# Maxima of the scores by quarters of k, and fourteen more pairs of them in the front

## The chip, the cores and the metric

One core of a Trainium2 chip runs the whole program in one launch. The metric is the device time of that core in microseconds. The engines are TensorE (PE in the profile; PEld is its weight load), VectorE (DVE), ScalarE (ACT), GpSimd (POOL) and SyncE (SP), which here only issues DMAs.

## The reference

Two mixers of the same shape run on two inputs, and a gate per row mixes them. `A` is the real part of a two-dimensional Fourier transform, written as products with DFT matrices; `B` is full attention with 32 heads of 16 dimensions. S is 2048, D is 512, all in float32.

```python
x = A_x                                                   # [1, 2048, 512]
g = sigmoid((x * gate_w).sum(-1, keepdims=True))
a = einsum("bsd,ed->bse", x, dft_hid_re)
b = einsum("bsd,ed->bse", x, dft_hid_im)
y = einsum("ts,bse->bte", dft_seq_re, a) - einsum("ts,bse->bte", dft_seq_im, b)

q, k, v = (B_x @ wqkv) split into 32 heads of 16
p = softmax(einsum("bhqd,bhkd->bhqk", q, k) * 16 ** -0.5)
o = einsum("bhqk,bhkd->bhqd", p, v) @ wo
return g * y + (1 - g) * o
```

`B_x` and `A_x` come from the same draw, so both mixers work on one x. The weights `wqkv` and `wo` are drawn 64 times larger than the rest. So the scores are large, and the softmax needs the true maximum of each row before the exponential.

## The kernel before

**Number format and halves of the array.** Most products are taken in a format that keeps part of the mantissa, with each operand split into a high and a low part (`hi_lo`), so one product becomes three matmuls. The attention products and the DFT products contract over 64 rows of the array. Two such matmuls run at the same time, one on the upper and one on the lower half of the array. I call one such pair of 64-row matmuls a slot.

**Pairs of heads.** The 32 heads are handled as NP = 16 pairs. The rows of q and k of pair p stand in `qs[p % 2]` and `ks[p % 2]`, one head in partitions 0 to 63, the other in 64 to 127. `load_rows(p, c, cols)` brings them from DRAM with three DMAs on SP's queue, `load_q` does that for q and clears (for p > 1) the rows that will take the negated maxima.

**Two passes over the scores.** The first pass, `a_tile`, computes a tile of 128 queries by 512 keys on TensorE and DVE reduces it to one maximum per query (L246 and L248). There are 64 such tiles for each pair and head: 16 query blocks times 4 quarters of k. They run with the query block outside and the quarter inside. When the tiles of eight query blocks of both heads are done, `m_parts` reduces the four maxima of each query and splits them, and `m_rows` transposes them (L267) and stores them by DMA as extra rows of `qs`, four DMAs on SP and four on POOL. The second pass, `scores` (L788), then multiplies k with those extended rows, so that the product already has the maximum subtracted, and ACT takes the exponential (L789). A unit u is one block of 128 keys of one pair for one half of the queries; there are 32 units per pair and 512 in all. `values` multiplies the exponentials of two units with v (`pv`, L824). One ACT copy takes the sum out, and POOL adds it up.

**The front.** Stage 1 (up to 93 us of the profile) computes q and k for all heads and stores them in DRAM. Then come four rows of v alone (L362) and the fours: `four` computes four blocks of 128 rows with 48 matmuls in each, in four phases of twelve slots (L344). In phases 0 and 1 each block gets one half of its contraction, in phases 2 and 3 the other, in the other half of the array. The first matmul of phases 2 and 3 waits for a maximum of the phase before (`guard`). There are three fours for v, four fours for b (the imaginary part along the hidden dimension), and one at `wre` for the first rows of a. In the first seven, `maxima` puts a pair of tiles, one for each head, behind the products 3 and 8 of each phase. That is 8 pairs in a four and `LEAD` = 56 in all. In the four at `wre`, `first_tiles` puts in scores and maxima. Banks of PSUM are taken in turn: four for the products of a four (`"s"`), and the other three and `psD` for the tiles (`"a"`).

**The segments.** From 209 us on, the work is written out as segments. A pattern is a string of slots: `s` is a score tile and `a` a tile of maxima, on one half of the array, while the other half works on a product of the DFT or of the output projection; a letter pair such as `aS` has tiles on both halves and no product. At `|` the plan is run, and the values of two units follow. Each pattern runs twice, with the halves exchanged, and the chains of products use `psD`. The order is 24 segments of `THIN` (the rest of a), 192 of `FULL` (the DFT along the sequence), and then the patterns of the projection: 14 segments of `FOURTEEN`, 2 of `TWELVE` and 16 of `TEN`, and the end.

```python
    FULL = "s a s s a a s s a a s a s a a s |"
    THIN = "aS s a s a s s a s a s a a sA |"
    FOURTEEN = ("aS s aS s a s ^ a s a s a sA |",) * 2
    TWELVE = ("sA a s a s ^ s a s a s s a s |",) * 2
    TEN = "aA s s a s ^ s s s a a sS |", "a s a sS a ^ s s s s s aA |"
```

In `FULL` a segment has eight scores and eight maxima; in `FOURTEEN` seven maxima, in `TWELVE` six and in `TEN` five. So the maxima keep their lead over the scores up to the projection, and it runs down there. The banks of score and maxima tiles come from a planner (`bank`, `read_by`), which guesses when each of seven banks will be free and takes the earliest; its first guesses are the list `free[:]` behind the four at `wre`.

**The plan.** `at(u, f, ...)` puts a step down for the end of the segment at which the values have come to unit u. The loads of pair p stand there relative to u = 32 * (p - 1): before the change q's first half 12 units ahead, the first half of k 6 ahead, the rest of k 4 and 2 ahead (the last quarter for each head by itself) and q's second half 2 ahead. DMAs issued by SP leave in program order, the loads of the DFT matrices (`c_load`, L392) among them.

Of the kernel before, what the change touches and what calls it, by code (L numbers as in the profile page):

```python
# [10 lines left out]
F32 = mybir.dt.float32  # L11
# [5 lines left out]
P = 128  # L17
S = 2048
D = 512
H = 32  # L20
DH = 16
NP = H // 2
KT = D // P
NT = S // P
UNITS = NP * 32
LEAD = 56
RAW = 6
PSUM = bass.MemoryType.PSUM
DRAM = bass.MemoryType.DRAM
# [3 lines left out]
def mix_kernel(ctx: ExitStack, tc: tile.TileContext, xa_t, xa, wqkv, w_hid, w_seq, wo, gate_w, out):  # L33
# [40 lines left out]

    xab = [const.tile([P, 4, 2, D], F32R, name=f"xab{tb}", tag=f"xab{tb}") for tb in range(4)]

    turns = dict.fromkeys("fsa", 0)

    def turn_of(kind):

        group = {"f": banks, "s": banks[:4], "a": [*banks[4:], psD]}[kind]
        turns[kind] += 1
        pool = group[(turns[kind] - 1) % len(group)]
        return pool.tile([P, 512], F32, name="d" if pool is psD else "t")
# [125 lines left out]

    PARTS = (0, 0, 1), (0, 1, 0)

    def load_rows(p, c, cols, heads=(0, 1)):


        t = (qs, ks)[c][p % 2]
        h0, n = heads[0], len(heads)
        rows = slice((2 * p + h0) * DH, (2 * p + h0 + n) * DH)
        for i, v in enumerate(PARTS[c]):
            nc.sync.dma_start(t[64 * h0 + i:64 * (h0 + n):4, cols].bitcast(F32), qk_d[c][v, rows, cols])  # L220

    def clear(t, rows, cols):
        dst = t[rows, cols].bitcast(F32).rearrange("r (n c) -> r n c", c=P)
# [6 lines left out]
            clear(qs[p % 2], slice(3, P, 32), cols)  # L230

    LOW, HIGH = slice(0, S // 2), slice(S // 2, S)
    THIRD, LAST = slice(S // 2, 3 * S // 4), slice(3 * S // 4, S)
    ALL = slice(0, S)


# [2 lines left out]

    def a_tile(i, h, ps=None):  # L240
        p, j = divmod(i, 64)
        qt, kb = divmod(j, 4)
        if ps is None:
            ps = turn_of("a")
        r = slice(64 * h, 64 * h + 64)
        nc.tensor.matmul(ps, qs[p % 2][r, qt * P:(qt + 1) * P], ks[p % 2][r, kb * 512:(kb + 1) * 512],  # L246
                         start=True, stop=True)
        user = nc.vector.tensor_reduce(mx[p % 2][:, h, qt, kb:kb + 1], ps, AX.X, ALU.max)  # L248
        n = 4 if p == NP - 1 and j >= 32 else 8
        k = qt // n  # L250
        a_left[p, n, k] = a_left.get((p, n, k), 8 * n) - 1
        if not a_left[p, n, k]:
            deferred.extend((partial(m_parts, p, n, k), partial(m_rows, p, n, k)))
        return user
# [24 lines left out]
    ones = st1.tile([4, 2 * D], F32, name="hl", bufs=2)  # L279
    nc.gpsimd.memset(ones, 1.0)  # L280
    for i in range(2):
        (nc.gpsimd if i else nc.vector).memset(ks[i].bitcast(F32), 0.0)
        nc.gpsimd.memset(qs[i].bitcast(F32), 0.0)
        if i == 0:
            load_rows(0, 1, ALL)
            load_q(0, ALL)
            nc.gpsimd.memset(vt[:, :, :, 16:17], 1.0)
        for tb in range(2):
            nc.gpsimd.dma_start(ks[i][3:P:32, tb * 2 * D:(tb + 1) * 2 * D].bitcast(F32), ones)
# [13 lines left out]
    def v_done(s, ps):  # L303

        pv = ps.rearrange("p (r h d) -> p r h d", h=2, d=DH)
        nc.scalar.copy(vt[:, s, :, 0:16], pv[:, :, 0])
        nc.vector.tensor_copy(vt[:, s, :, 17:33], pv[:, :, 1])
        if s in range(6, 14, 2):
            kt = (s - 6) // 2
            wt = st1.tile([P, 2, D], F32R, name="hl", bufs=2)  # L310
            hi_lo(wt[:, 0], wt[:, 1], wos.pop(0), nc.gpsimd)
            nc.sync.dma_start(wo_d[kt], wt.bitcast(F32))
            wrs.append(staged(w_hid[0, :, kt]))
# [19 lines left out]
    def four(ss, wh, wl, done, between=None):  # L333

        ps = [turn_of("s") for _ in ss]
        seen = None
        for phase, pair in enumerate(((0, 1), (2, 3), (1, 0), (3, 2))):
            guard, seen = seen, None
            both = [row_products(ss[c], wh, wl) for c in pair]
            for j in range(12):  # L340
                for half, c in enumerate(pair):
                    st, mv = next(both[half])
                    r = slice(64 * half, 64 * half + 64)
                    i = nc.tensor.matmul(ps[c], st[r], mv[r], start=phase < 2 and j == 0, stop=phase > 1 and j == 11)  # L344
                    if phase > 1 and j == 0:
                        tc.add_manual_dep(
                            i.ins, guard.ins.name,
                            mybir.DependencyInfo(mybir.DependencyClass.Sync, mybir.DependencyReason.DATA))
                if j in (3, 8):
                    user = between(phase, j) if between else maxima()  # L350
                    seen = seen or user
            if deferred:
                deferred.pop(0)()
            if phase > 1:
                for c in sorted(pair):
                    done(ss[c], ps[c])
# [417 lines left out]
    def scores(u, qb, h, ps=None):  # L774
        p, r = divmod(u, 32)
        hf, kt = divmod(r, 16)
        q0 = hf * 1024 + qb * 512
        if u >= UNITS - 16:

            blk, kt = divmod(kt, 8)  # L780
            q0, kt = 1024 + blk * 512, 2 * kt + qb
        if u not in pts:
            pts[u] = work.tile([P, 4, 512], F32, name="pt", bufs=4)
        if ps is None:
            i, ps = bank()
            read_by(i, "s")
        rr = slice(64 * h, 64 * h + 64)
        nc.tensor.matmul(ps, ks[p % 2][rr, kt * P:(kt + 1) * P], qs[p % 2][rr, q0:q0 + 512], start=True, stop=True)  # L788
        return nc.scalar.activation(pts[u][:, 2 * qb + h], ps, AF.Exp, bias=0.0, scale=DH ** -0.5)  # L789
# [94 lines left out]
    def at(u, f, *args):  # L884
        plan.setdefault(u, []).append(partial(f, *args))

    for p in range(2, NP):
        u = 32 * (p - 1)
        at(u - 12, load_q, p, LOW)
        at(u - 6, load_rows, p, 1, LOW)  # L890
        if p > 2:
            at(u - 4 if p < NP - 1 else u - 2, load_rows, p, 1, LAST, (1,))
        at(u - 4, load_rows, p, 1, THIRD)
        at(u - 2, load_rows, p, 1, LAST, (0,))
        at(u - 2, load_q, p, HIGH)

    for hf in range(2):
# [30 lines left out]

    FULL = "s a s s a a s s a a s a s a a s |"
    THIN = "aS s a s a s s a s a s a a sA |"  # L930
    FOURTEEN = ("aS s aS s a s ^ a s a s a sA |",) * 2
    TWELVE = ("sA a s a s ^ s a s a s s a s |",) * 2
    TEN = "aA s s a s ^ s s s a a sS |", "a s a sS a ^ s s s s s aA |"

# [31 lines left out]
    def segment(pattern, half, ds, stop, between=None, hold=True):  # L966


        nonlocal now
        nonlocal users  # L970
        before, users = users, []
        ds, late = iter(ds), []
        back = late if hold else None
        for n, slot in enumerate(pattern.split()):
            if slot == "|":
                for f in late:
                    f()
# [12 lines left out]
            if ahead:  # L990
                score(slot[0], 1 - half)
            if len(slot) == 1:
                x = next(ds, None)
                if x:

                    before = before if x[0].begun else None
                    i = issue(x, half, stop, back)
                    users = []
                    if before:
                        tc.add_manual_dep(  # L1000
                            i.ins, dict(before[::-1]).get("s", before[0][1]).ins.name,
                            mybir.DependencyInfo(mybir.DependencyClass.Sync, mybir.DependencyReason.DATA))
                        before = None
            if not ahead and slot != "d":
                score(slot[0], 1 - half)
            if len(slot) == 2:
                score(slot[1].lower(), half)
            if n == 1 and valued == 30:
                load_rows(2, 1, LAST, (1,))
        if deferred:  # L1010
            deferred.pop(0)()

    def pairs():

        for i in range(NT - 4):
            yield (THIN,) * 2, take(hid, 12)
        for i in range(2 * NT * 3):
            yield (FULL,) * 2, take(seq, 16)
        for patterns, n in ((FOURTEEN, 7), (TWELVE, 1), (TEN, 8)):
            for i in range(n):  # L1020
                yield patterns, take(both_first, 9)

# [14 lines left out]
    def first_tiles(phase, j):  # L1037

        if j == 3:
            user = scores(*next(streams[0][0]), turn_of("a"))  # L1040
            a_tile(*next(streams[1][1]))
            return user
        for h in range(2):
            a_tile(*next(streams[h][1]))

    four(range(4), *wre, first_rows, first_tiles)
    free[:] = 0.0, 0.0, 4.0, 4.0, 1.0, 2.0, 3.0
# [59 lines left out]
```

## Time and profile before

| | us |
|---|---|
| median of 3 runs | 1673.14 (1672.26 to 1673.52) |
| the profiled execution | 1673.48 |
| its span, first to last instruction | 1671.6 |
| TensorE busy | 1661.8 (99% of the span) |
| DVE busy | 1379.8 (83%) |
| ACT busy | 1245.5 (75%) |
| POOL busy | 754.4 (45%) |
| granted TensorE clock | 0.999 |

The span is the time from the first to the last instruction in the profile, and the rest of the time lies around it. A share is an average over stages: front (104 to 197 us for the seven fours), THIN up to about 343 us, FULL up to about 1456 us, and the patterns of the projection behind it. What a change is worth is read stage by stage. In the chain that ended last, each row gives its start, its length and the work it belongs to; the rows of L824 mark the ends of segments.

### The profile page before, as it was taken

Reading aid. Unit: us, or ns where it says so; the run is one execution under the profiler, and the core shown is the slowest. Engines: PE = TensorE matmul, PEld = TensorE weight load, DVE = VectorE, ACT = ScalarE, POOL = GpSimd, SP = SyncE. Lnnn points to the kernel's source line nnn. Section 1 sums busy time; section 2 is a strip of 40 time slices with the busy share of each in tenths; the row PEclk is TensorE's granted clock in tenths of the full one; section 3 lists DMA queues with packets and bytes.
Section 4 is the critical chain, followed back from the end, with each engine's and each line's share of the span. In section 5 each row is a group of like instructions: output and inputs, shape, how many; then the busy total and the mean of one; then the engine's idle time right before and its main releaser. Section 6 shows DMA issues by size and latency. Waiting matters only on the chain.

```text
span 1671.6 us, 34975 instructions
## 1 busy us (share of the span) xinstructions
PE 1661.8 (99%) x13170; PEld 1000.6 (60%) x13170; DVE 1379.8 (83%) x2299; ACT 1245.5 (75%) x2470; POOL 754.4 (45%) x813
## 2 busy tenths in 40 slices
PE   9999999999999999999999999999999999999998
PEld 7889966655555555555555555555555555555554
DVE  5468788888888888888888888888888888888786
ACT  5212288887777788777777788777787788888995
POOL 1123644544444465454444556545455465422331
PEclk9999999999999999999999999999999999999999
DMA  9953401113121323212226333222232334531113
GB/s 302 338 156 133 164 2 38 29 49 87 53 64 56 87 80 118 68 59 65 74 80 239 95 103 110 77 68 75 55 99 57 89 112 118 196 129 32 23 51 134
DMA packets 88833, 165.65 MB, mean 99 GB/s; under 512 B 21056, under 2 KB 22472, under 8 KB 87512
## 3 DMA queue, kind: packets, MB, share of 16 engines
q1 hardware_dynamic: 84024, 162.63, 30.9%
q8 instruction: 104, 1.70, 0.4%
q0 software_dynamic: 4352, 0.39, 0.2%
q14 instruction: 65, 0.53, 0.1%
q10 hardware_dynamic: 288, 0.39, 0.1%
HBM read 107.73 MB, written 54.52 MB: 97 GB/s over the span
## 4 chain that ended last, share of the span: by engine, by line
PE 98%; DMA 1%; DVE 0%; SPq 0%; ACT 0%; issue 0%; DVEq 0%
PE d L457 36%; PE t L824 28%; PE t L246 12%; PE t L788 10%; PE t L344 5%; PE t L93 2%; PE t L91 2%; PE t L92 2%; PE t L805 1%; PE t L457 1%; DMA qs<-qk 0%; DMA raw<-wqkv 0%; DVE mx L248 0%; PE t L183 0%; DVE yp L649 0%; SPq L220 0%
## 5 line engine op out<-in xcount | busy, mean ns | idle before, releaser
L248 DVE TENSOR_REDUCE mx<-t 128x1 f32<-128x512 f32 x2016 | 1253.6, 684 | 217.6 <-PE t L246 178.9
L789 ACT ACTIVATE pt<-t 128x512 f32<-128x512 f32 x2048 | 1033.9, 632 | 9.9 <-PE t L788 9.5
L788 PE MATMUL t<-qs,ks 64*128 64x512 f32 x2048 | 739.9, 410 | 0.1
L246 PE MATMUL t<-ks,qs 64*128 64x512 f32 x2016 | 687.5, 398 | 1.0 <-DMA qs<-qk 1.0
L457 PE MATMUL d<-xab,ch 64*128 64x512 f32 x2016 | 656.0, 400 | 0.0
L824 PE MATMUL t<-pt,vt 128*32 128x512 f32 x3968 | 477.1, 598 | 0.0
L457 PEld LDWEIGHTS d<-xab,ch 64*128 64x128 f32 x2016 | 357.9, 184 | 141.8 <-issue 97.2
L246 PEld LDWEIGHTS t<-ks,qs 64*128 64x128 f32 x2016 | 365.3, 184 | 86.3 <-ACT pt L789 47.4
L788 PEld LDWEIGHTS t<-qs,ks 64*128 64x128 f32 x2048 | 369.0, 184 | 76.4 <-DVE mx L248 43.7
L457 PE MATMUL d<-xab,cl 64*128 64x512 f32 x1008 | 403.6, 400 | 0.0
L839 POOL TENSOR_TENSOR osum<-osum,oe 128x512 f32<-128x512 f32 x217 | 279.5, 1288 | 134.3 <-ACT oe L833 131.0
L833 ACT COPY oe<-t 128x512 f32<-128x512 f32 x217 | 127.4, 587 | 223.9 <-PE t L824 222.3
L824 PEld LDWEIGHTS t<-pt,vt 128*32 128x32 f32 x3968 | 103.6, 109 | 231.6 <-issue 148.9
L402 POOL CAST ch<-craw 128x512 fp32r<-128x512 f32 x126 | 77.3, 613 | 340.8 <-PE t L788 266.0
L457 PEld LDWEIGHTS d<-xab,cl 64*128 64x128 f32 x1008 | 185.7, 184 | 72.3 <-issue 50.3
L403 POOL TENSOR_TENSOR cl<-craw,ch 128x512 fp32r<-128x512 f32 x126 | 162.3, 1288 | 10.2
L271 POOL DMA_DIRECT2D qs<-mt x132 | 73.6, 563 | 98.4 <-DVE mt L267 82.4
L457 PE MATMUL d<-wo_hl,o_hl 64*128 64x512 f32 x288 | 76.5, 394 | 0.0
L457 PE MATMUL d<-wre,xab 64*128 64x512 f32 x288 | 70.0, 389 | 0.4 <-DVE mx L248 0.4
L457 PEld LDWEIGHTS d<-wo_hl,o_hl 64*128 64x128 f32 x288 | 51.3, 184 | 10.2 <-ACT pt L789 6.7
L457 PEld LDWEIGHTS d<-wre,xab 64*128 64x128 f32 x288 | 53.0, 184 | 3.8 <-DVE mx L248 0.8
L91 PE MATMUL t<-xab,wh 128*128 128x512 f32 x124 | 48.2, 389 | 0.0
(118 smaller groups left out, 951.2 us busy)
## 6 DMA issues: line engine op xcount, KB each, us to landing
craw<-w_seq SPq DMA_DIRECT2D x128, 256.0 KB
qk<-hl SPq DMA_DIRECT2D x32, 512.0 KB
qs<-qk SPq DMA_DIRECT2D x84, 128.0 KB
b<-hl SPq DMA_DIRECT2D x16, 512.0 KB
xab<-b SPq DMA_DIRECT2D x16, 512.0 KB
o<-osum SPq DMA_DIRECT2D x62, 128.0 KB
oh<-nh SPq DMA_DIRECT2D x12, 512.0 KB
o_hl<-oh SPq DMA_DIRECT2D x6, 1024.0 KB
```

Source lines behind the costliest of these rows:

```text
L91: nc.tensor.matmul(ps, sh, mh, start=first, stop=False)
L246: nc.tensor.matmul(ps, qs[p % 2][r, qt * P:(qt + 1) * P], ks[p % 2][r, kb * 512:(kb + 1) * 512], start=True, stop=True)
L248: user = nc.vector.tensor_reduce(mx[p % 2][:, h, qt, kb:kb + 1], ps, AX.X, ALU.max)
L344: i = nc.tensor.matmul(ps[c], st[r], mv[r], start=phase < 2 and j == 0, stop=phase > 1 and j == 11)
L402: nc.gpsimd.tensor_copy(h1, raw)
L403: nc.gpsimd.tensor_tensor(l1, raw, h1.bitcast(F32), ALU.subtract)
L457: i = nc.tensor.matmul(self.ps, st[r], mv[r], start=not self.begun, stop=stop)
L788: nc.tensor.matmul(ps, ks[p % 2][rr, kt * P:(kt + 1) * P], qs[p % 2][rr, q0:q0 + 512], start=True, stop=True)
L789: return nc.scalar.activation(pts[u][:, 2 * qb + h], ps, AF.Exp, bias=0.0, scale=DH ** -0.5)
L824: nc.tensor.matmul(acc[32 * j:32 * j + 32], vt[:, kt, p, h:h + 32], pt[:, j], start=u == us[0], stop=u == us[-1])
L833: nc.scalar.copy(oe, acc)
L839: nc.gpsimd.tensor_tensor(o, o, oe, ALU.add)
```

## The change

Six things change together.

1. `a_tile` runs the tiles with the quarter of k outside and the query block inside, over groups of eight query blocks (four in the second half of the last pair).
2. The loads of k go by quarters of the keys, both heads together: the quarters 14, 10, 6 and 2 units ahead. q's first half is loaded 14 units ahead in place of 12.
3. In the seven fours, the pairs of maxima stand behind the products 2 and 7 of phase 0, 1, 5 and 10 of phases 1 and 3, and 3 and 8 of phase 2. That is 10 pairs in a four, and `LEAD` is 70. With those of the four at `wre`, the lead at the first segment is 74 tiles for one head and 78 for the other.
4. In the projection, the 14 segments of `FOURTEEN` go, and 14 more of `TEN` come: 2 of `TWELVE`, then 30 of `TEN`.
5. The tiles in the four at `wre` take three banks in turn, without `psD`.
6. The second copy of v leaves DVE for ACT, and of the first two memsets of `ks` and `qs`, `ks` goes to POOL and `qs` to DVE.

```diff
-LEAD = 56
+LEAD = 70
...
-        group = {"f": banks, "s": banks[:4], "a": [*banks[4:], psD]}[kind]
+        group = {"f": banks, "s": banks[:4], "a": [*banks[4:], psD], "r": banks[4:]}[kind]
...
-    def load_rows(p, c, cols, heads=(0, 1)):
+    def load_rows(p, c, cols):
         t = (qs, ks)[c][p % 2]
-        h0, n = heads[0], len(heads)
-        rows = slice((2 * p + h0) * DH, (2 * p + h0 + n) * DH)
+        rows = slice(2 * p * DH, 2 * (p + 1) * DH)
         for i, v in enumerate(PARTS[c]):
-            nc.sync.dma_start(t[64 * h0 + i:64 * (h0 + n):4, cols].bitcast(F32), qk_d[c][v, rows, cols])
+            nc.sync.dma_start(t[i:P:4, cols].bitcast(F32), qk_d[c][v, rows, cols])
...
     def a_tile(i, h, ps=None):
         p, j = divmod(i, 64)
-        qt, kb = divmod(j, 4)
+        n = 4 if p == NP - 1 and j >= 32 else 8
+        k, j = divmod(j, 4 * n)
+        kb, qt = divmod(j, n)
+        qt += n * k
...
     for i in range(2):
-        (nc.gpsimd if i else nc.vector).memset(ks[i].bitcast(F32), 0.0)
-        nc.gpsimd.memset(qs[i].bitcast(F32), 0.0)
+        nc.gpsimd.memset(ks[i].bitcast(F32), 0.0)
+        (nc.gpsimd if i else nc.vector).memset(qs[i].bitcast(F32), 0.0)
...
         nc.scalar.copy(vt[:, s, :, 0:16], pv[:, :, 0])
-        nc.vector.tensor_copy(vt[:, s, :, 17:33], pv[:, :, 1])
+        nc.scalar.copy(vt[:, s, :, 17:33], pv[:, :, 1])
...
-                if j in (3, 8):
+                if j in (((2, 7), (1, 5, 10), (3, 8), (1, 5, 10))[phase] if not between else (3, 8)):
                     user = between(phase, j) if between else maxima()
...
     for p in range(2, NP):
         u = 32 * (p - 1)
-        at(u - 12, load_q, p, LOW)
-        at(u - 6, load_rows, p, 1, LOW)
-        if p > 2:
-            at(u - 4 if p < NP - 1 else u - 2, load_rows, p, 1, LAST, (1,))
-        at(u - 4, load_rows, p, 1, THIRD)
-        at(u - 2, load_rows, p, 1, LAST, (0,))
+        at(u - 14, load_q, p, LOW)
+        for kb in range(4):
+            at(u - 14 + 4 * kb, load_rows, p, 1, slice(kb * 512, (kb + 1) * 512))
         at(u - 2, load_q, p, HIGH)
...
-            if n == 1 and valued == 30:
-                load_rows(2, 1, LAST, (1,))
...
-        for patterns, n in ((FOURTEEN, 7), (TWELVE, 1), (TEN, 8)):
+        for patterns, n in ((TWELVE, 1), (TEN, 15)):
...
         if j == 3:
-            user = scores(*next(streams[0][0]), turn_of("a"))
-            a_tile(*next(streams[1][1]))
+            user = scores(*next(streams[0][0]), turn_of("r"))
+            a_tile(*next(streams[1][1]), turn_of("r"))
             return user
         for h in range(2):
-            a_tile(*next(streams[h][1]))
+            a_tile(*next(streams[h][1]), turn_of("r"))
```

More of the change, by code (lines that the diff above doesn't have):

```diff
@@ L75, in mix_kernel @@
     xab = [const.tile([P, 4, 2, D], F32R, name=f"xab{tb}", tag=f"xab{tb}") for tb in range(4)]
-    turns = dict.fromkeys("fsa", 0)
+    turns = dict.fromkeys("fsar", 0)
     def turn_of(kind):
-        group = {"f": banks, "s": banks[:4], "a": [*banks[4:], psD]}[kind]
+        group = {"f": banks, "s": banks[:4], "a": [*banks[4:], psD], "r": banks[4:]}[kind]
         turns[kind] += 1
@@ L232, in mix_kernel @@
     LOW, HIGH = slice(0, S // 2), slice(S // 2, S)
-    THIRD, LAST = slice(S // 2, 3 * S // 4), slice(3 * S // 4, S)
     ALL = slice(0, S)
@@ L248, in a_tile @@
         user = nc.vector.tensor_reduce(mx[p % 2][:, h, qt, kb:kb + 1], ps, AX.X, ALU.max)
-        n = 4 if p == NP - 1 and j >= 32 else 8
-        k = qt // n
         a_left[p, n, k] = a_left.get((p, n, k), 8 * n) - 1
@@ L930, in mix_kernel @@
     THIN = "aS s a s a s s a s a s a a sA |"
-    FOURTEEN = ("aS s aS s a s ^ a s a s a sA |",) * 2
     TWELVE = ("sA a s a s ^ s a s a s s a s |",) * 2
```

## The prediction

> **What bounds the kernel now.** I read the page first (busy times and the chain that ended last), then that chain in order of time to get the period of each stage, then DVE's timeline where a stage is longer than its matmuls, and last the timelines of the entry of the front and of the load queue.
>
> ```profile
> span 1671.6 us, 34975 instructions
> ...
> PE 1661.8 (99%) x13170; PEld 1000.6 (60%) x13170; DVE 1379.8 (83%) x2299; ACT 1245.5 (75%) x2470; POOL 754.4 (45%) x813
> ...
> PE 98%; DMA 1%; DVE 0%; SPq 0%; ACT 0%; issue 0%; DVEq 0%
> ...
> L248 DVE TENSOR_REDUCE mx<-t 128x1 f32<-128x512 f32 x2016 | 1253.6, 684 | 217.6 <-PE t L246 178.9
> ...
> L246 PE MATMUL t<-ks,qs 64*128 64x512 f32 x2016 | 687.5, 398 | 1.0 <-DMA qs<-qk 1.0
> ```
>
> TensorE issues all the time, so a gain comes only where its stream is stretched: by empty half-slots, or by a matmul that waits for a bank. The chain gives the stretch stage by stage. A slot here is one pair of 64-row matmuls, one on each half of the array.
>
> ```profile
> 125.71 0.23 PE t L246 x2
> 125.94 1.13 PE t L344 x10
> ...
> 128.89 0.23 PE t L246 x2
> ...
> 190.49 0.23 PE t L246 x2
> ...
> 192.12 1.64 PE t L344 x14
> 193.76 0.23 PE t L246 x2
> ```
>
> In the front a phase is 12 product slots and 2 maxima slots. In the three v fours it lasts 128.89 - 125.71 = 3.18 us and a slot 1.13 / 5 = 0.226 us; in the four b fours 3.27 us and 1.64 / 7 = 0.234 us. There are no holes: the front runs at its matmuls.
>
> ```profile
> 1450.14 1.85 PE t L824 x16
> 1455.95 1.85 PE t L824 x16
> ...
> 1482.98 1.85 PE t L824 x16
> ...
> 1531.25 1.85 PE t L824 x16
> ...
> 1541.49 1.85 PE t L824 x16
> 1546.25 1.88 PE t L824 x16
> ...
> 1574.96 1.87 PE t L824 x16
> ```
>
> Each row is the block of value products that ends a segment, so differences are segment periods. FULL: 5.81 us for 16 slots. FOURTEEN, the 14 segments from 1455.95 to 1531.25: 75.30 us, 5.38 each, for 12 slots. TWELVE: (1541.49 - 1531.25) / 2 = 5.12. TEN: (1574.96 - 1546.25) / 6 = 4.785 for 11 slots. FOURTEEN has four slots fewer than FULL and gains only 0.43 us; by FULL it should take 5.81 - 4 x 0.226 = 4.91. Something else stretches it, and DVE's timeline shows what:
>
> ```profile
> 1479.94 4.28 DVE L248 TENSOR_REDUCE mx<-t 128x1 f32<-128x512 f32 x7 [0.42 <-PE t L788]
> 1485.29 4.28 DVE L248 TENSOR_REDUCE mx<-t 128x1 f32<-128x512 f32 x7 [1.07 <-PE t L788]
> 1489.48 0.74 DVE L649 SCALAR_TENSOR_TENSOR yp<-d,omg,yp 128x512 f32<-128x512 f32 x1
> ```
>
> Seven maxima run back to back for 4.28 us, while the slots of that segment need only 5.38 less the 1.85 of the value block, 3.5. DVE is the limit inside the slots and idles (1.07 us) during the value block; TensorE waits for banks in between. TEN has five maxima (about 3.1 us) and lacks this wait. The same rows give DVE's pace: (4.28 - 0.68) / 6 = 0.60 us from one maximum to the next.
>
> **Part 1: fourteen pairs of maxima go to the front, FOURTEEN becomes TEN.** Each of the seven fours gets 10 pairs in place of 8, so LEAD goes from 56 to 70, and seven pairs of FOURTEEN segments (7 maxima per half) become TEN (5 per half): 14 pairs either way. In the tail, 14 TEN segments take 14 x 4.785 = 66.99 in place of 75.30: **-8.31 us**. At the least it saves the bare slot, 14 x 0.226 = 3.2, if the wait seen in FOURTEEN stays. I take the full figure since TEN ran at 4.785 from its first segments on, right behind TWELVE, and will again.
>
> In the front, TensorE pays the slots: 6 pairs x 0.226 + 8 x 0.234 = **+3.23 us**. That holds only if DVE keeps up. A v four will have 58 slots, 13.1 us, a b four 13.6; DVE has 20 maxima x 0.60 = 12.0. The copies of the v fours would not fit beside that:
>
> ```profile
> L307 DVE COPY vt<-t x16: 415/420/425, 98.9 to 145.0; 128x256 f32<-128x256 f32 x16
> ...
> L306 ACT COPY vt<-t x16: 379/388/391, 98.5 to 144.2; 128x256 f32<-128x256 f32 x16
> ```
>
> Four of 0.42 us in a four make 13.7, over the 13.1; the change gives them to ACT, where eight copies of 0.39 are 3.1 us in 13.1, so they cost nothing (left on DVE, about 3 x 0.6 = 1.8 us). The third pair is spread well: pairs are 5 to 7 slots apart, at worst 1.13 us against 1.20 of DVE work, and 7 slots follow. Each bank is used again two pairs later, at least 11 slots or 2.49 us, while a pair's second maximum ends about 0.43 + 0.60 + 0.68 = 1.7 us after its matmul (0.43 is the lag from a matmul to its maximum that DVE's rows show above, 0.42). The first product of phases 2 and 3 waits for the first pair of the phase before, 10 slots earlier: 2.27 against 1.7. What eats into this slack is the group maximum and its transpose, now twice inside the front:
>
> ```profile
> L259 DVE TENSOR_REDUCE nm<-mx x33: 186/209/220, 157.5 to 1629.3; 128x16 f32<-128x64 f32 x31, 128x8 f32<-128x32 f32 x2
> ...
> L267 DVE STREAM_TRANSPOSE mt<-nhl x33: 201/202/213, 161.2 to 1630.1; 128x32 f32<-128x32 f32 x33
> ```
>
> 0.41 us of lag per group against a slack of 0.6 to 0.8. I book **+0.3 us** for the front, between 0 and 0.8 (both groups in full). Their row stores (four DMAs on SP, four on POOL for each group) come earlier, too; POOL has room for the second group, which falls into the last b four:
>
> ```profile
> L271 POOL DMA_DIRECT2D qs<-mt x132 | 73.6, 563 | 98.4 <-DVE mt L267 82.4
> ...
> 193.59 0.61 POOL L320 CAST hl<-raw 128x512 fp32r<-128x512 f32 x1 [4.43 <-ACT raw L318]
> ```
>
> Four issues of 0.56 make 2.3 us beside an idle spell of 4.43, and the eviction behind them (b_done on POOL) holds no bank.
>
> A page of the Trainium skill speaks against this: "VectorE: DVE Perf Modes", section "The DRAIN you can't avoid", says that a VectorE operation does not start before the one ahead of it has emptied the pipe. With 684 ns for each maximum that would make 13.7 us of DVE per four, above TensorE's 13.1 and 13.6. This trace differs: seven maxima of 684 ns in 4.28 us overlap by about 0.08 each. I go by the trace and keep the rule as a rival.
>
> **Part 2: the entry of the front.** The two memsets ahead of the loads of pair 0 change engines.
>
> ```profile
> 93.21 1.81 POOL L283 MEMSET qs<- 128x2048 f32 x1 [41.31 <-PE t L92]
> ...
> 95.71 1.76 DVE L282 MEMSET ks<- 128x2048 f32 x1 [0.38 <-DMA qk<-hl]
> 97.50 1.80 SPq L220 DMA_DIRECT2D ks<-qk  x3
> ...
> 99.40 1.81 SPq L220 DMA_DIRECT2D qs<-qk  x3
> ...
> 104.18 1.20 PE L344 MATMUL t<-wv,xab 64*128 64x512 f32 x8
> ...
> 106.36 0.50 PE L246 MATMUL t<-ks,qs 64*128 64x512 f32 x2 [0.98 <-DMA qs<-qk]
> ```
>
> SP issues the k loads at 97.50, when DVE's memset of k ends (97.47), and the q loads behind them. DVE reaches that memset only after its evictions and gate rows, while POOL has stood idle for 41 us and starts at 93.21. With k on POOL, k is clear at 95.0 and its loads go out from about 95.1 (SP's last store before them is then out); q, cleared by DVE, is ready at 97.5. The last q load then leaves 1.9 us earlier, and if it lands as long after its issue as now, the first pair's data is there at about 104.4. TensorE gets there at 104.18 + 3 slots = 104.9 and today waits from 105.09 to 106.36: **-1.27 us**, at worst 0 if k's memory is not free before 95.7. Behind the two memsets POOL has the ones of vt, which wait for a store anyway.
>
> **Part 3: the entry of the segments.**
>
> ```profile
> 207.72 0.39 PE L246 MATMUL d<-ks,qs 64*128 64x512 f32 x1
> ...
> 208.57 0.39 PE L788 MATMUL t<-qs,ks 64*128 64x512 f32 x1
> ...
> 209.43 0.49 PE L457 MATMUL d<-wre,xab 64*128 64x512 f32 x1 [0.42 <-DVE mx L248]
> ```
>
> The first chain of the segments (L457) needs psD, which the last maximum of the four at wre (the d of 207.72) holds until DVE has read it; unhindered it would start a slot behind 208.57, at 208.80, 0.63 earlier. With three banks in turn psD is free. But 16 tiles over three banks end on the first of them, and the planner gives just that bank to the next score. That score will wait for the same maximum, so the wait moves down by one matmul: **-0.3 us**, between 0 and -0.63.
>
> **Part 4: order of maxima and loads of k.** The same 64 maxima per pair and head run, and the groups of eight query blocks complete at the same counts; only the inner order changes. k of a pair came in 12 loads (six of them just ahead of its use); now it comes in 12, three for each quarter, at 14, 10, 6 and 2 units ahead, all on SP, and each set waits for the last score on the quarter that it overwrites. Behind that wait on SP's queue stand the chunk loads of the DFT.
>
> ```profile
> 833.15 17.39 SPq L220 DMA_DIRECT2D ks<-qk  x9
> 850.64 0.53 SPq L392 DMA_DIRECT2D craw<-w_seq  x1
> ...
> 855.09 0.39 PE L246 MATMUL t<-ks,qs 64*128 64x512 f32 x1
> ```
>
> Today such a wait also lasts (nine loads spread over 17.39 us, a chunk load behind them), and no chunk is late. The third quarter, issued by 850.54, is read at 855.09 without a wait: it lands within 4.6 us. After the change the first maximum of a pair runs third in the third segment behind the load, 1.85 + 2 x 5.81 + about 1.4 = 14.9 us later; q's four loads (rows and clear) and the three of k take 7 x 0.62 = 4.3 to issue, so 8.9 to land: 6 us to spare. **0 us**, and if the cover fails the rival below tells the price. FULL keeps its patterns, and its 16 slots at 0.226 plus the value block and 0.3 between them make its 5.81, so I leave it there.
>
> **Sum.** -8.31 + 3.23 + 0.3 - 1.27 - 0.3 = -6.35 us against the profiled execution, 1673.48 us (span 1671.6 and 1.9 around it): 1667.1. The median of the runs shown is 0.34 below that execution: **1666.8 us**. With the best ends (0 for the front's lag, -1.27, -0.63) it is 1666.2; with both entries bringing nothing and 0.8 of lag it is 1668.9.
>
> **The rivals.**
>
> *DVE bounds the front* (the DRAIN rule at work as a mechanism: each maximum holds DVE for its 684 ns). Seven fours at 20 x 0.684 = 13.7 make 95.8 us, where the slots make 3 x 13.1 + 4 x 13.6 = 93.7: +2.1, so 1668.9. For it: six maxima in an odd phase are more than its slack allows one by one. Against it: the 4.28 us row. Chance 0.13.
>
> *The tail does not follow*: TEN brought forward runs into what stretches FOURTEEN, such as late projection operands, and only the bare slots are saved (3.2, not 8.3): 1666.8 + 5.1 = 1671.9, within 0.2% of no change. For it: the loads of the last DFT tile end just there. Against it: FOURTEEN's waits are for DVE, none for a load. Chance 0.12.
>
> *Slower: k's quarters come late.* Today's reader of a new pair is eight units later. If the landing takes over 14.9 us, q's loads being ahead of k's on SP, TensorE waits once in each of the 14 pairs from 2 to 15; the gain is gone at 6.35 / 14 = 0.45 us per pair, and it is slower by over 0.2% from 0.7 us on; a wait of 1.5 us gives 1666.8 + 21 = 1687.8. For it: the queue holds waits up to 17 us. Against it: 4.6 us to land, and only 1.0 us of waiting for loads in all of L246. Chance 0.11.
>
> **Numbers.** What is left, 0.64, is for the sum as it stands. Measurement of this kernel tells about 0.2%, 3.3 us, from no change. Faster by more takes the main case and most of the DVE rival (1668.9 is 4.2 under the median): 0.64 + 0.12 = 0.76; same takes the second rival and the rest: 0.13; slower 0.11. The range goes from 1664.8 (the best ends, less 1.4 for FULL periods that shift by 0.007 us over 192 segments) to 1670.0 (the DVE rival with 0.8 of lag, rounded up).
>
> **What would show it.** Right: b phases with two and three pairs alternate at 3.28 and 3.51 us without a DVE release in the chain; value blocks of the tail 4.785 apart from the third segment on; k loads issued near 95; no DMA in the chain at 105. Wrong: DVE mx L248 in the chain of the front, waits of L246 for qs<-qk once a pair, a FULL period other than 5.81, or tail segments over 5.

## The result: 1669.1 us in place of 1672.8, three fifths of the forecast gain

| | before | after |
|---|---|---|
| median of 13 runs each, us | 1672.78 (1671.93 to 1674.05) | 1669.10 (1668.11 to 1671.40) |
| span of the profiled execution, us | 1671.6 | 1667.9 |

The ratio is 0.9978, with a 95% interval of 0.9969 to 0.9986. So the changed kernel is faster, by 3.7 us. The forecast was 1666.8 us with a range of 1664.8 to 1670.0, and a gain of 6.35 us.

The first view of the changed kernel is its page: span, busy times, shares of the chain that ended last, and the group of the matmuls of the maxima (busy time and mean ns of one, then the idle time ahead of them with what ended most of it).

```profile
span 1667.9 us, 34971 instructions
...
PE 1658.0 (99%) x13170; PEld 984.6 (59%) x13170; DVE 1374.9 (82%) x2283; ACT 1251.0 (75%) x2486; POOL 753.4 (45%) x813
...
PE 98%; DVE 0%; POOL 0%; DMA 0%; issue 0%; SPq 0%; DVEq 0%; ACT 0%
...
L247 PE MATMUL t<-ks,qs 64*128 64x512 f32 x2013 | 675.6, 399 | 1.6 <-POOL qs L282 1.6
```

The shares say nothing about the difference: TensorE is still 99% busy. But one word is new. In the kernel before, the matmuls of the last row waited 1.0 us for a load of q. Now they wait 1.6 us for something on POOL. That leads to the step that failed.

The stage table is worked out from the chains of the two profiled executions, from one landmark to the next.

| stage, us | before | after | difference | forecast |
|---|---|---|---|---|
| up to the rows of v | 93.21 | 93.42 | +0.21 | 0 |
| rows of v | 10.97 | 10.97 | 0 | 0 |
| first product of the fours to the first pair of maxima | 2.17 | 2.53 | +0.36 | -1.27 |
| first pair to the first score of the segments | 102.21 | 105.51 | +3.30 | +3.53 |
| first score to the first block of values | 4.41 | 4.49 | +0.08 | -0.3 |
| `THIN` | 128.00 | 127.97 | -0.03 | 0 |
| `FULL` | 1114.90 | 1115.50 | +0.60 | 0 |
| the 32 segments of the projection | 162.67 | 154.50 | -8.17 | -8.31 |
| end | 53.04 | 53.05 | +0.01 | 0 |
| sum | 1671.59 | 1667.95 | -3.64 | -6.35 |

One slot has moved between two of these rows. The first pair of maxima stands behind four slots of products in the kernel before and behind three in the changed one. With that slot (0.23 us) taken into account, the way to the first pair grew by 0.59 and the stage behind it by 3.07.

The two large terms came out nearly as forecast. The tail is in the chain of the changed kernel, whose rows L823 end the segments:

```profile
1460.47 1.85 PE t L823 x16
...
1465.67 1.85 PE t L823 x16
...
1470.79 1.85 PE t L823 x16
...
1475.54 1.88 PE t L823 x16
```

Two segments of `TWELVE` take 5.20 and 5.12 us, and the first `TEN` behind them 4.75. From there on they are 4.785 apart, and 4.84 to 4.87 where a group maximum falls in. The last but one takes 5.21. That is what `TEN` took before (there the last but one took 5.20), now 30 times.

The front in the same chain, for ten pairs of maxima of a v four and then ten of a b four:

```profile
123.31 0.23 PE t L247 x2
...
136.46 0.23 PE t L247 x2
...
176.65 0.23 PE t L247 x2
...
190.11 0.23 PE t L247 x2
```

A v four takes 136.46 - 123.31 = 13.15 us and a b four 190.11 - 176.65 = 13.46, for 58 slots each. That is 0.227 and 0.232 a slot, and no row of DVE stands between them in the chain. DVE's timeline shows how close it is:

```profile
131.35 1.98 DVE L249 TENSOR_REDUCE mx<-t 128x1 f32<-128x512 f32 x3
133.24 0.68 DVE L249 TENSOR_REDUCE mx<-d 128x1 f32<-128x512 f32 x1
133.84 1.98 DVE L249 TENSOR_REDUCE mx<-t 128x1 f32<-128x512 f32 x3
135.74 0.68 DVE L249 TENSOR_REDUCE mx<-d 128x1 f32<-128x512 f32 x1
136.72 1.89 DVE L249 TENSOR_REDUCE mx<-t 128x1 f32<-128x512 f32 x3 [0.30 <-PE t L247]
```

Eight maxima take from 131.35 to 136.42, which is 0.63 each, and one starts before the one ahead of it ends (133.24 against 133.33). DVE hardly rests: in the three v fours together it waits 1.0 us for TensorE. And TensorE's waits show none for DVE in these fours.

The entry of the front went the other way. This is the timeline of the changed kernel (start, length, engine and line, and in brackets the idle time before with what ended it):

```profile
93.42 1.81 POOL L281 MEMSET ks<- 128x2048 f32 x1 [40.67 <-PE t L92]
...
94.96 0.36 SPq L144 DMA_DIRECT2D qk<-hl  x1
95.43 1.81 SPq L219 DMA_DIRECT2D ks<-qk  x3
...
95.92 1.76 DVE L282 MEMSET qs<- 128x2048 f32 x1 [0.38 <-issue]
97.71 1.72 SPq L219 DMA_DIRECT2D qs<-qk  x3
...
100.75 0.59 POOL L286 MEMSET vt<- 128x256 f32 x1 [5.52 <-DMA ks<-qk]
...
101.27 1.28 POOL L288 DMA_DIRECT2D ks<-hl  x2
...
106.93 0.50 PE L247 MATMUL t<-ks,qs 64*128 64x512 f32 x2 [1.57 <-POOL qs L282]
```

The loads of k leave at 95.43 and those of q at 97.71, as forecast (2.1 and 1.7 us earlier than before). But POOL then stands still for 5.52 us, until it clears `vt`, and behind that memset it issues the stores of ones into `ks` (L288), which the first pair of maxima needs as well. The same rows of the kernel before:

```profile
98.42 0.59 POOL L287 MEMSET vt<- 128x256 f32 x1 [3.40 <-DMA qk<-hl]
...
99.00 1.29 POOL L289 DMA_DIRECT2D ks<-hl  x2
```

There the ones left at 99.00, now at 101.27. The last row of the fence above names POOL's memset of `qs` as what released the first pair. That memset clears the other pair's `qs` and ended at 106.13, 0.8 us before the pair started, so another release is meant. The landing of the ones is the candidate, since the pair starts 5.7 us behind their first issue and the trace gives their two DMAs a median of 5.3 us from issue to landing; the first experiment tries it. What POOL waits for ahead of the memset of `vt` is named as a load of k here, and as the store `qk<-hl` in the kernel before and in the next two profiles quoted below. I take it to be the store, which the memset waits for in the kernel before too.

### The profile page after: what moved, and what is told of

The parts are those of the page before. It is cut to its first block, busy times and chain, and to the rows that moved or that the text cites. A ratio compares the mean times of both kernels' runs of the same rounds, so it can differ in the third digit from the quotient of the medians.

```text
span 1667.9 us, 34971 instructions
## 1 busy us (share of the span) xinstructions
PE 1658.0 (99%) x13170; PEld 984.6 (59%) x13170; DVE 1374.9 (82%) x2283; ACT 1251.0 (75%) x2486; POOL 753.4 (45%) x813
## 4 chain that ended last, share of the span: by engine, by line
PE 98%; DVE 0%; POOL 0%; DMA 0%; issue 0%; SPq 0%; DVEq 0%; ACT 0%
PE d L456 37%; PE t L823 28%; PE t L247 12%; PE t L787 9%; PE t L343 5%; PE t L93 2%; PE t L92 2%; PE t L91 2%; PE t L804 1%; PE t L456 1%; DMA ks<-qk 0%; PE t L161 0%; PE t L183 0%; DVE mx L249 0%; DVE yp L648 0%; PE t L733 0%
## 5 line engine op out<-in xcount | busy, mean ns | idle before, releaser
L787 PE MATMUL t<-qs,ks 64*128 64x512 f32 x2048 | 728.7, 408 | 0.4 <-DVE mx L249 0.2
L247 PE MATMUL t<-ks,qs 64*128 64x512 f32 x2013 | 675.6, 399 | 1.6 <-POOL qs L282 1.6
L823 PE MATMUL t<-pt,vt 128*32 128x512 f32 x3968 | 477.1, 598 | 0.0
L247 PEld LDWEIGHTS t<-ks,qs 64*128 64x128 f32 x2013 | 359.8, 184 | 84.2 <-ACT pt L788 55.9
L823 PEld LDWEIGHTS t<-pt,vt 128*32 128x32 f32 x3968 | 103.6, 109 | 232.1 <-issue 148.7
```

What stands on the lines that cost most here:

```text
L823: nc.tensor.matmul(acc[32 * j:32 * j + 32], vt[:, kt, p, h:h + 32], pt[:, j], start=u == us[0], stop=u == us[-1])
```

## Experiments

**The ones.** My theory after the result: the first pair waits for the stores of ones, and those stand on POOL behind the memset of `vt`, which waits for the last store of the stage before (`qk<-hl`). Put behind the ones, that memset costs nothing. The rival: the loads themselves land later, and the wait stays.

```diff
         if i == 0:
             load_rows(0, 1, ALL)
             load_q(0, ALL)
-            nc.gpsimd.memset(vt[:, :, :, 16:17], 1.0)
         for tb in range(2):
             nc.gpsimd.dma_start(ks[i][3:P:32, tb * 2 * D:(tb + 1) * 2 * D].bitcast(F32), ones)
+        if i == 0:
+            nc.gpsimd.memset(vt[:, :, :, 16:17], 1.0)
```

> The changed kernel, with the memset of the ones in vt put behind the two stores of ones into ks of pair 0 on POOL's queue. Theory: the first pair of maxima waits for these stores, which stand on POOL behind the vt memset, and that memset waits until the last store of stage 1 has landed (100.7). Then the stores leave near 95.3, the first pair runs at about 105.2 without a wait in place of 106.93, and all behind it is 1.7 us earlier. Rival: the loads of k and q themselves land late, because they now share the DMA engines with the last store; then the first pair stays at 106.9 and nothing is gained.

```profile
95.30 1.81 SPq L219 DMA_DIRECT2D ks<-qk  x3
...
95.41 1.29 POOL L287 DMA_DIRECT2D ks<-hl  x2 [0.30 <-POOL ks L281]
...
100.47 0.58 POOL L289 MEMSET vt<- 128x256 f32 x1 [3.78 <-DMA qk<-hl]
...
105.06 0.40 PE L247 MATMUL t<-ks,qs 64*128 64x512 f32 x2
```

This is its timeline. The ones leave at 95.41, the memset of `vt` still waits until 100.47, and the first pair runs at 105.06 without a wait. From the first product of the fours to the first pair it is 0.80 us, in place of 2.53, and 2.17 in the kernel before. The time was 1667.62 us. So the theory holds. Against the kernel before that is -1.37 as the rows stand and -1.14 with the moved slot, so Part 2 of the prediction (-1.27) would have been nearly right if this memset had not been in the way.

Timed over several runs, the same edit:

> The kernel of the run with the vt memset behind the stores of ones, timed against the kernel before. Theory: 1.7 us from the entry on top of the changed kernel, so about 5.4 us under the kernel before (ratio 0.9968); the profile shows the first pair at 105.2 at the latest. Rival: the single run was lucky in the landing of its loads, and the median stays within 0.7 us of the changed kernel (ratio 0.9974 to 0.9978).

1667.50 us, median of 7 runs (1666.86 to 1667.85), against 1672.57 for the kernel before on that chip; the ratio is 0.997 with an interval of 0.9958 to 0.9981. The wait of the first pair is again 0.80. This is the best version that I ran: 5.1 us under before. The interval overlaps that of the changed kernel (0.9969 to 0.9986), so that it is faster than that one rests on the entry in the profiles more than on these times.

**The swap of the memsets, undone.** With the old engines for `ks` and `qs`, first with the memset of `vt` where the change has it, then with it behind the ones.

```diff
-        nc.gpsimd.memset(ks[i].bitcast(F32), 0.0)
-        (nc.gpsimd if i else nc.vector).memset(qs[i].bitcast(F32), 0.0)
+        (nc.gpsimd if i else nc.vector).memset(ks[i].bitcast(F32), 0.0)
+        nc.gpsimd.memset(qs[i].bitcast(F32), 0.0)
```

> The changed kernel, with the first two memsets on the engines of before (ks on DVE, qs on POOL). Theory (stores of ones behind the vt memset): k's loads leave at 97.5 again, out of the way of the last store, which then lands near 98.4; the stores of ones follow at once, and the first pair runs at 106.3 to 106.6, 0.3 to 0.6 us earlier than in the changed kernel. Rival (the loads are the limit): k's loads leave 2.1 us later, so the first pair comes no earlier than 106.9 and rather later.

```profile
97.65 1.80 SPq L219 DMA_DIRECT2D ks<-qk  x3
98.58 0.59 POOL L286 MEMSET vt<- 128x256 f32 x1 [3.41 <-DMA qk<-hl]
...
99.16 1.28 POOL L288 DMA_DIRECT2D ks<-hl  x2
...
99.55 1.81 SPq L219 DMA_DIRECT2D qs<-qk  x3
...
105.61 0.50 PE L247 MATMUL t<-ks,qs 64*128 64x512 f32 x2 [0.31 <-DMA qs<-qk]
```

The first pair ran at 105.61, earlier than any theory had it. Loads that leave 2 us later landed early enough: in the chain, the last load of q takes 4.71 us to land here and 5.60 in the kernel before. In all 1668.23 us, from one run.

> The changed kernel with the vt memset behind the stores of ones and with the first two memsets on the engines of before. Theory: with the stores of ones out of the way the first pair waits for the loads, and these leave 2 us later when DVE clears k; so the first pair runs 0.4 to 1.3 us after TensorE could take it (between 105.5 and 106.4), where the kernel with the vt memset alone had no wait. Rival: the swap of the memsets does nothing once the stores of ones are early; the first pair then runs without a wait here too, about 0.8 us after the first product of the fours.

```profile
98.31 1.29 POOL L287 DMA_DIRECT2D ks<-hl  x2 [3.06 <-DVE ks L281]
...
99.63 1.81 SPq L219 DMA_DIRECT2D qs<-qk  x3
...
106.06 0.51 PE L247 MATMUL t<-ks,qs 64*128 64x512 f32 x2 [0.68 <-DMA qs<-qk]
```

Here the wait is for the loads of q, and the entry takes 1.65 us; in all 1668.59. The four combinations, with the time from the first product of the fours to the first pair in every profile that had that entry (some from the experiments below). The numbers marked with a star have four slots of products ahead of the pair, the others three:

| | memsets as before | memsets swapped |
|---|---|---|
| `vt` ahead of the ones | 2.17\*, 1.23\*, 1.74\*, 1.41\*, 1.28 | 2.53, 1.74, 2.00, 1.59 |
| `vt` behind the ones | 1.65 | 0.80, 0.80, 0.80 |

With 0.23 taken off the starred numbers for the slot that the others have behind the pair, the means of the upper row are 1.38 and 1.96. So by themselves the swapped memsets bring nothing and seem to cost 0.6, though the spreads overlap. Together with the earlier ones they bring about 0.85 (1.65, from one profile, to 0.80). And the spread of the starred numbers, 0.94 us with one and the same entry, says that my -1.27 was taken from a single landing at its slow end. Where the landing of q's last load stands in the chain with that entry, it takes 5.60, 5.17 and 4.84 us, and 5.60 is the profile that I had.

**Order of maxima and loads alone.** The kernel before, with the new order of tiles and loads by quarters only.

```diff
-        qt, kb = divmod(j, 4)
+        n = 4 if p == NP - 1 and j >= 32 else 8
+        k, j = divmod(j, 4 * n)
+        kb, qt = divmod(j, n)
+        qt += n * k
...
-        at(u - 12, load_q, p, LOW)
-        at(u - 6, load_rows, p, 1, LOW)
...
+        at(u - 14, load_q, p, LOW)
+        for kb in range(4):
+            at(u - 14 + 4 * kb, load_rows, p, 1, slice(kb * 512, (kb + 1) * 512))
```

> The kernel before, with only the order of the maxima (quarter by quarter over eight query blocks) and the loads of k by quarters at 14, 10, 6 and 2 units ahead; lead 56, FOURTEEN, memsets and copies as before. Theory: order and loads cost nothing by themselves; the stage FULL lasts 1114.9 us as before (within 0.1), no maximum waits for a load after the entry, and the whole is within 0.5 us of the kernel before. Rival: the order or the loads bring the two segments of 6.09 us that FULL shows in the changed kernel; then FULL is longer by about 0.56 here too.

1672.91 us, against 1672.57 for the kernel before beside it; `FULL` takes 1114.97 (before 1114.90), the 32 segments 162.58 (162.67). Part 4's 0 us holds for the reordering. One segment of `FULL` takes 6.09 us here, as two do in the changed kernel, and yet `FULL` as a whole grew by 0.07 only.

**The cover of the loads.** Is it 0 because the loads are hidden, or because such a load never matters? The changed kernel with k's loads four units later:

```diff
-            at(u - 14 + 4 * kb, load_rows, p, 1, slice(kb * 512, (kb + 1) * 512))
+            at(u - 10 + 4 * kb, load_rows, p, 1, slice(kb * 512, (kb + 1) * 512))
```

> The changed kernel, with the four loads of each pair's k four units later (10, 6, 2 units ahead and 2 behind), that is two segments or 11.6 us later. Theory: the cover of 14.9 us falls to 3.3 us, while three issues and the landing take about 1.9 + 4.6 = 6.5; the first maximum of a pair waits about 3 us, in most of the 14 pairs and again at later quarters, so the whole is 30 to 100 us slower. Rival: the loads land much faster than the bound of 4.6 us, and the loss stays under 10 us.

1711.72 us, inside the range that I had given; `FULL` grew by 43. The view of waits (engine, what it waited for, total us, times, longest) and two rows of the chain (start, length, what):

```profile
PE t L247 <- DMA ks<-qk: 25.9, 12, 2.8
```

```profile
492.24 2.52 DMA ks<-qk
...
680.22 2.24 DMA ks<-qk
```

So the slower rival's mechanism is real, and four units of lead stand between it and this kernel.

**The copies of v.** The changed kernel with the second copy of v left on DVE.

```diff
-        nc.scalar.copy(vt[:, s, :, 17:33], pv[:, :, 1])
+        nc.vector.tensor_copy(vt[:, s, :, 17:33], pv[:, :, 1])
```

> The changed kernel, with the second copy of v on DVE again, as before. Theory: DVE then has 20 x 0.60 + 4 x 0.42 = 13.7 us in a v four against 13.15 of slots; the three v fours take about 13.7 us each, 1.6 to 1.8 us more in all, with waits for mx in the chain. Rival: the copies run in gaps and four banks absorb the rest; the v fours stay at 13.15 us and nothing is lost.

1669.31 us. The front took 106.49 in place of 105.51, so the copies cost 0.98 us there, where I had said about 1.8. Its chain shows the place:

```profile
131.51 0.31 PE d L247
...
135.76 0.31 PE t L247 x2
```

A second tile that normally adds 0.01 us now adds 0.31. In the three v fours the weight loads of the maxima wait for DVE's maxima five times, 1.2 us in all, and never in the changed kernel. Sign and mechanism were right; DVE had more slack than I gave it.

**Which bank the first score takes.** In Part 3 I had the wait of the first chain move to the next score, which needs the same bank. Here the planner's first guesses give it another.

```diff
-    free[:] = 0.0, 0.0, 4.0, 4.0, 1.0, 2.0, 3.0
+    free[:] = 0.0, 0.0, 4.0, 4.0, 3.0, 1.0, 2.0
```

> The changed kernel, with the planner's first guesses changed so that the first bank of three, which the last maximum of the four at wre holds, is handed out last of the three (3, 1, 2 in place of 1, 2, 3). Theory: the wait moved from the chain's bank to the score's bank; then the score at 213.29 runs about 0.4 us earlier, and the way from the first score of the segments to the first value block falls from 4.49 us to about 4.0. Rival: DVE is behind by then in any case, and the wait moves on to the next tile: 4.4 to 4.5 us as in both kernels.

1668.74 us. From the first score to the first values it takes 4.46 in place of 4.49, so nothing was won: another wait, for DVE and then for ACT, takes its place. The chain of the changed kernel itself shows the wait that I had described:

```profile
211.82 0.10 PE t L247
...
211.95 1.30 DVE mx L249 x2
...
213.29 0.50 PE t L787
```

**What stretches `FOURTEEN`.** The prediction says DVE. The kernel before, with the maxima of these 14 segments taken over 256 of the 512 keys only:

```diff
-        user = nc.vector.tensor_reduce(mx[p % 2][:, h, qt, kb:kb + 1], ps, AX.X, ALU.max)
+        src = ps[:, :256] if short[0] else ps
+        user = nc.vector.tensor_reduce(mx[p % 2][:, h, qt, kb:kb + 1], src, AX.X, ALU.max)
...
+        short[0] = patterns is FOURTEEN
```

> The kernel before, with the maxima of the FOURTEEN segments taken over 256 of the 512 keys of a tile only (that part of the maxima is left out), so that each holds DVE for about 0.33 us in place of 0.60. Theory: FOURTEEN is stretched by tiles waiting for a bank that DVE still reads; with short maxima its period falls from 5.35 to 4.8 to 4.95 us, by 5.5 to 7.5 us over 14 segments. Rival: it is stretched by its pattern of slots on TensorE or by ACT; then it stays over 5.2 us.

1669.55 us. The 14 segments went from 75.30 to 72.22, a gain of 3.08 and well under what I expected; each still takes 5.16 in the chain. In these segments the weight loads of the maxima waited 11.4 us for DVE's maxima before, and 0.8 now. The timeline shows DVE resting and weight loads of the scores held by ACT:

```profile
1478.01 2.30 DVE L250 TENSOR_REDUCE mx<-t 128x1 f32<-128x256 f32 x5 [1.18 <-PE t L790]
...
1478.16 4.03 ACT L791 ACTIVATE pt<-t 128x512 f32<-128x512 f32 x8
...
1480.28 0.18 PEld L790 LDWEIGHTS t<-qs,ks 64*128 64x128 f32 x1 [0.19 <-ACT pt L791]
```

So the long maxima account for 3.08 of the 8.31 us by which the prediction has `FOURTEEN` above `TEN`. Another 3.2 is the bare slot that `FOURTEEN` has more (14 x 0.226), and about 2.0 are left. ACT was the next suspect: eight exponentials in 4.03 us and one copy of 0.59 make 4.62 in each segment. I moved that copy to DVE, on top of the short maxima, in `FOURTEEN` and `TEN`:

```diff
-        nc.scalar.copy(oe, acc)
+        (nc.vector.tensor_copy if on_dve[0] else nc.scalar.copy)(oe, acc)
...
+        on_dve[0] = patterns is FOURTEEN or patterns is TEN
```

> The kernel of the short maxima (before, with the maxima of FOURTEEN over 256 of 512 keys, the rest left out), and in FOURTEEN and TEN the copy of the value sums goes from ACT to DVE. Theory: what still stretches FOURTEEN there (5.15 us) and sets TEN (4.785) is ACT, with eight exponentials and one copy; without the copy ACT can start its exponentials earlier, and FOURTEEN falls to 4.85 to 4.95, TEN to 4.5 to 4.65. Rival: TensorE's own slots and the value block are the limit; both periods stay within 0.05.

1673.04 us. `FOURTEEN` fell to 71.22 only, 1.0 us less over 14 segments, and `TEN` rose from 4.785 to 5.03. The theory that ACT's share is what is left asked for 3 to 4 us in `FOURTEEN` and a shorter `TEN`, so it fell. The same copy moved in `TEN` alone, on the version with the memset of `vt` behind the ones:

> The changed kernel with the vt memset behind the stores of ones, and with the copy of the value sums on DVE in the TEN segments (30 of them). Theory (ACT limits TEN): each TEN segment is 0.13 to 0.28 us shorter, 4 to 8 us in all on top of the kernel with the vt memset alone, so 9 to 13 us under the kernel before (ratio 0.992 to 0.9945). Rival (slots limit TEN, or DVE's copy now holds the bank of a maximum): TEN stays at 4.785 or grows, ratio 0.997 or above.

1673.90 us, median of 11 runs; ratio to before 1.0009 (1.0000 to 1.0018), so all of the gain is gone. `TEN` takes 5.02. DVE's and then ACT's timeline:

```profile
1540.07 0.69 DVE L834 COPY oe<-t 128x512 f32<-128x512 f32 x1
1540.68 3.15 DVE L250 TENSOR_REDUCE mx<-t 128x1 f32<-128x512 f32 x5
```

```profile
1540.70 4.03 ACT L790 ACTIVATE pt<-t 128x512 f32<-128x512 f32 x8 [1.06 <-PE t L789]
```

The copy now stands ahead of five maxima on DVE. ACT, free of it, starts its exponentials no earlier: it idles 1.06 us until TensorE has a score for it. Taking work off a busy engine doesn't help where that engine's next input is what is late. Why the segment grew is argued: the copy's 0.69 us ahead of the maxima on DVE fits, and no run takes the copy off ACT without putting it there.

## Why the prediction was right and wrong

**Part 1 was right in both terms.** The tail brought -8.17 (forecast -8.31), and the front cost +3.30, or +3.07 for the 14 pairs alone (forecast +3.23 in slots and 0.3 of lag, the lag not seen). I had put the lag at 0.3 for the two group maxima; no row of DVE is in the front's chain. One figure in that part held by luck: the 0.43 from a matmul to its maximum was read off a row that gives an idle time of DVE, 0.42. In the first experiment the first maximum does start 0.44 behind its matmul (105.50 and 105.06). The rival of a DVE-bound front is out: 20 maxima fit into 13.15 us, where 684 ns for each would make 13.7. So the rule of the Trainium skill ("VectorE: DVE Perf Modes", section "The DRAIN you can't avoid") doesn't hold for these maxima, and the section itself excepts a next operation that isn't held. The same page, in the section "Two Vector instructions with no wait between them", lets an operation that isn't held start before the one ahead has ended, and the trace agrees with that: 133.24 against 133.33 above. By that page an operation is held, in the main, when its operands start in another group of 32 partitions than those of the operations before it.

My reason for the tail was only half right. `FOURTEEN` isn't long for DVE alone. Of the 8.3 us, 3.2 are the slot that it has more than `TEN`, 3.08 came back with half-length maxima, and about 2.0 are not explained; moving the copy off ACT brought 1.0 of them. What carried the forecast was the row of `TEN` itself, 4.785 measured in the same kernel, and not the mechanism.

**Part 2 failed.** The step "Behind the two memsets POOL has the ones of vt, which wait for a store anyway" stopped one instruction too early. Behind the ones of `vt` are the stores of ones into `ks`, and the first pair waits for those. As the loads of k left 2.1 us earlier, POOL's wait ahead of the memset ended 2.3 us later (100.75 against 98.42), and the ones left as much later. Instead of -1.27 the entry brought +0.36 in the profiled execution, and +0.59 with the moved slot; over all profiles with either entry it is about the same, +0.58 (1.96 against 1.38), with spreads that overlap. Of the 2.7 us between forecast and result this is 1.9.

**Part 3 failed by its size.** The wait moved down to the next score, as I wrote, but nothing was gained: +0.08 where I took -0.3, outside the bounds of 0 and -0.63. With another bank the next wait takes over (4.46).

**Part 4** held for the loads and the order. `FULL`, which I left at zero, grew by 0.60. Two of its 192 segments take 6.09 us in place of 5.81, which makes 0.56 of it. One of them is here:

```profile
797.88 1.85 PE t L823 x16
...
803.96 1.85 PE t L823 x16
...
809.77 1.85 PE t L823 x16
```

In ACT's timeline the copy behind the value block comes late just there. The block from 797.88 ends at 799.73 and its copy starts 0.40 us later; the block from 803.96 ends at 805.82 and its copy starts after 0.12, as in every segment of `FULL` but the two. The 0.28 between them is what the segment takes more:

```profile
800.13 0.59 ACT L832 COPY oe<-t 128x512 f32<-128x512 f32 x1 [1.00 <-PE t L823]
...
805.94 0.59 ACT L832 COPY oe<-t 128x512 f32<-128x512 f32 x1 [1.29 <-PE t L823]
```

They are the same two segments in six of the experiments that have the whole change or nearly so. With the copies of v on DVE there are two others, with the order alone one, and none in the kernel before. So it goes with the program more than with chance. Why is open; no run tries it.

The other terms nearly cancel: +0.38 from Part 3, +0.21 ahead of the rows of v, which the change doesn't touch, and +0.14 in the tail stand against -0.46 in the front. With 1.9 from Part 2 and 0.6 from `FULL` they make the 2.7.

That the time still lies in the range is partly luck. The forecast's poor end for its own sum, with nothing from both entries and 0.8 of lag, was 1668.9, and the measured 1669.1 lies above it. The room up to 1670.0 was set aside for a DVE-bound front, which didn't come; two losses that I hadn't allowed for, a slower entry and a longer `FULL`, used it.

## What to carry to other kernels

When a load is brought forward, follow every instruction behind it on each queue involved up to the one that the reader waits for, and ask what the earlier load does to stores still on their way. A wait of a microsecond that ends with one transfer's landing is worth less than it looks in a single profile, since landings vary; take it from several, or give it a wide range. For the price of a pattern, the same pattern measured elsewhere in the trace is better than a reason for why another one is slow.

## What the runs showed of the hardware

- A store on its way seems to be slowed by loads that start behind it, if the store is what POOL waits for. The last store of q and k was issued at 94.75 before, and POOL's wait for it ended at 98.42, 3.7 us later. After the change it was issued at 94.96, the loads of k followed at 95.43, and the wait ended at 100.75: 5.8 us. With the loads back at 97.65 it ended at 98.58. That the loads do it by taking the same DMA engines is argued, not tried.
- Maxima of 684 ns start 0.60 to 0.63 us apart when they run back to back (seven in 4.28 us, eight in 5.07), and 20 of them fit into a v four of 13.15 us in which TensorE doesn't wait for them.
- An engine's share of a segment doesn't tell whether relief helps: ACT had 4.62 us of work in a 4.785 us segment, and with a copy of 0.59 moved from ACT to DVE the segment took 5.02.
